# First-tile normalisation on VectorE, spread modulation products and zero matmuls, in the opening of an adaLN + linear attention + SwiGLU kernel

## The chip, the cores and the metric

The kernel runs on one core of a Trainium2 chip. The metric is the device time of one execution in microseconds (us), as a median over runs. The span of a profile, counted from its first instruction, is 1.7 to 2.1 us shorter than the time of the same execution. For most runs the span and the mean granted TensorE clock (as the profiler records it: 1.0 is full speed, 0.5 half) were recorded too.

A ratio of two kernels below is the mean time of one kernel's fast runs over that of the other's of the same rounds, so it is not quite the ratio of the medians that are quoted. "Fast" is a coarse label here: a run is called slow only from 1.5% above the fastest.

## The reference, cut to what matters

```python
mod = (_silu(c) @ w_mod).reshape(c.shape[0], 6, 1, -1)
sa, ca, ga, sb, cb, gb = (mod[:, 0].copy(), mod[:, 1].copy(), ...)
h = _layernorm(x, axis=-1) * (1 + ca) + sa      # x: 1 x 2048 x 1024, bf16
x = x + ga * _A_ref(h, A_wqkv, A_wo)            # q, k, v projections, linear attention, wo
h = _layernorm(x, axis=-1) * (1 + cb) + sb
x = x + gb * _B_ref(h, B_w_gate, B_w_up, B_w_down)
```

Only the first lines matter: before the first key projection, a row tile of `x` must be normalised, transposed and modulated with `ca` and `sa`, and those two are themselves products of a weight that has to be loaded.

## The kernel before: the parts the change touches

The first 512 rows are four row tiles of 128. Each gets statistics on VectorE (`ln_stats`), two small operations on GpSimd, a normalisation (`ln_xn`), eight transposes on TensorE (`tr0`), an evacuation (`tr0_evac`, a copy of the result out of PSUM, where the matmuls write) and a modulation on VectorE (`modulate`).

```python
def ln_xn(st, pool):
    rstd, nmr = stat.pop(st)
    if pool:
        nc.gpsimd.tensor_scalar(out=xns[st % 6], in0=xs[st % 6], scalar1=rstd[:], scalar2=nmr[:], ...)
    else:
        nc.scalar.activation(out=xns[st % 6], in_=xs[st % 6], func=ACT.Identity, scale=rstd[:], bias=nmr[:])
```

`ca` and `sa` are made in four blocks of two column chunks each ("modulation blocks"). A block is two products of 16 matmuls with one column each, kind 0 for `ca` and kind 1 for `sa`, written to columns of bank 7. Then come three small VectorE copies and the modulation of the two chunks. Only after that may the key matmuls of those chunks run. There are eight chunks (`cc`) and eight key groups; `kmm` is one 128x128 by 128x512 matmul. A zero matmul multiplies zeros; nobody uses its result.

```python
def mod_mm(kind, c0, c1):
    for cc in range(c0, c1):
        o = (2 * cc) + kind
        col = (0 if kind else D) + cc * P
        for j in range(DC):
            nc.tensor.matmul(bank[7][:, o:o + 1], lhsT=wme[:, j, col:col + P], rhs=scT[:, j:j + 1],
                             start=(j == 0), stop=(j == DC - 1))

def mod_pair(p):
    mod_mm(0, 2 * p, 2 * p + 2)
    mod_mm(1, 2 * p, 2 * p + 2)
    mod_rows(2 * p, 2 * p + 2)
...
warm(17)                       # zero matmuls, to raise the clock
for st in range(STC):
    ln_stats(st)
...
ln_xn(0, False); tr0(0); warm(3)
ln_xn(1, False); tr0(1); tr0_evac(0)
ln_xn(2, False); ln_xn(3, False)
...
tr0_evac(1); mod_pair(0); tr0(2); tr0_evac(2)
for cc in range(2):
    modulate(0, cc, saT, ca1T, 0, 2 * P)
...                            # key matmuls of chunks 0 and 1, tr0(3), mod_pair(1)
for p in (1, 2):
    for cc in (2 * p, 2 * p + 1):
        for g in range(7):
            kmm(bank[g], 0, G[g][0], G[g][1], cc)
            if p == 1 and cc == 3 and g == 2:
                mod_pair(2)
                for c_ in range(4, 6):
                    modulate(0, c_, saT, ca1T)
mod_pair(3)
for cc in range(6, 8):
    modulate(0, cc, saT, ca1T)
...                            # the 22 key matmuls that are left, then the value matmuls
```

The loads of `x` and of the weights go through one queue (SyncE's) in a fixed order: four row tiles, then modulation blocks alternating with key weights. In the timelines each engine runs its instructions in the order of the program.

## Time and profile before

| | us |
|---|---|
| median of 3 runs | 840.76 (840.35 to 841.16) |
| the profiled run itself | 842.11, span 840.2, mean clock 0.998 |
| TensorE busy | 827.6, 99% |
| value matmuls begin | 32.97 |

The page of before, its head and the busy line (engine, busy us, share of the span, instructions):

```profile
span 840.2 us, 10541 instructions
## 1 busy us (share of the span) xinstructions
PE 827.6 (99%) x4144; PEld 389.8 (46%) x4224; DVE 354.4 (42%) x663; ACT 155.0 (18%) x291; POOL 78.9 (9%) x147
```

TensorE is the limit. So a change of the opening is worth what it moves the start of the value matmuls by, and not more.

The chain of waits of before in its first 45 us (start, length, what), in part:

```profile
11.97 8.95 DMA M<-in_w_mod_dram
...
20.96 0.55 PE bank L391 x16
...
23.26 3.85 PE bank L271 x12
```

The chain reaches back from the second product of the third modulation block (20.96) to the load that it needs. The last line is twelve key matmuls that took 3.85 us.

TensorE in before, in order of time, in part. The columns are start, length, engine, line of the kernel, operation, output and inputs, shapes, count, and in brackets the idle time before the group and what ended it. `128x1` are the modulation products, `128x128` the transposes, L271 the key matmuls, L286 the value matmuls.

```profile
start us, us, engine line op out<-in xcount [idle before <-releaser]
...
11.81 1.03 PE L271 MATMUL bank<-M,M 128*128 128x512 bf16 x3
...
17.04 2.33 PE L271 MATMUL bank<-M,M 128*128 128x512 bf16 x10 [0.24 <-DVE M L253]
19.23 0.55 PE L391 MATMUL bank<-scT,M 128*128 128x1 bf16 x16
20.96 0.55 PE L391 MATMUL bank<-scT,M 128*128 128x1 bf16 x16 [1.18 <-DMA M<-in_w_mod_dram]
21.38 1.67 PE L271 MATMUL bank<-M,M 128*128 128x512 bf16 x5
23.26 3.85 PE L271 MATMUL bank<-M,M 128*128 128x512 bf16 x12 [0.22 <-issue]
...
32.97 1.24 PE L286 MATMUL bank<-M,M 128*128 128x512 bf16 x5
```

Matmuls overlap, so a group's length is not its count times the length of one. From group to group, one 512-column matmul takes about 0.216 us at full clock (for example the 22 key matmuls from 28.22 to 32.97, of which the trace has 21 records), and 0.43 us at half clock.

The windows of before around the DMA wait, TensorE alone (window, its length, busy us with instructions, granted clock, DMA share and GB/s):

```profile
core 0: us, PE busy (x), PEclk, DMA share, GB/s
...
18.63:22.04 3.41, 2.23 (x40) 1.00 1.13 326
22.04:25.45 3.41, 3.19 (x9) 0.50 1.07 314
```

One window of 3.41 us at clock 0.50 follows a window in which TensorE was busy for only 2.23 us. Twelve key matmuls at full clock would take about 2.6 us, so this group lost 1.3 us.

### The profile page before, as it was taken

What the parts mean: (1) busy time and instruction counts of PE and PEld (TensorE: products, weight loads), DVE (VectorE), ACT (ScalarE), POOL (GpSimd) and SP (SyncE); (2) the same over time, 40 slices, a digit from 0 to 9 for tenths busy, and PEclk for the clock granted to TensorE, in tenths of its full rate; (3) what the DMA queues carried; (4) which work ended last, traced back from release to release, by engine and by line L of the source; (5) the groups of instructions that cost most, each with busy time, mean ns of one, the idle gap of its engine ahead of it and who ended that gap; (6) DMA issues with size and microseconds to landing.
All of it is one profiled execution on the core that took longest, in us unless ns stands there. A gap on an engine that the chain in (4) does not pass through costs nothing.

```text
span 840.2 us, 10541 instructions
## 1 busy us (share of the span) xinstructions
PE 827.6 (99%) x4144; PEld 389.8 (46%) x4224; DVE 354.4 (42%) x663; ACT 155.0 (18%) x291; POOL 78.9 (9%) x147
## 2 busy tenths in 40 slices
PE   7999999999999999999999999999999999999998
PEld 3454554544444444444444444444444444444445
DVE  4668888788655656635341111111101211111111
ACT  4335533323211111111110001111000111100000
POOL 2034210022122323100000000000000000000000
PEclk9999999999999999999999999999999999999999
DMA  9985879055599889777874225555322555211210
GB/s 289 312 165 103 161 139 237 17 151 134 127 225 221 219 233 292 187 251 226 249 245 140 76 69 151 151 151 151 106 75 82 154 157 153 76 36 46 76 69 26
DMA packets 223009, 128.62 MB, mean 153 GB/s; under 512 B 76016, under 2 KB 209136, under 8 KB 222960
## 3 DMA queue, kind: packets, MB, share of 16 engines
q1 hardware_dynamic: 182112, 98.58, 43.0%
q10 hardware_dynamic: 38544, 20.98, 11.1%
q0 software_dynamic: 2304, 8.39, 2.6%
q8 instruction: 33, 0.54, 0.3%
q14 instruction: 16, 0.13, 0.1%
HBM read 97.52 MB, written 12.58 MB: 131 GB/s over the span
## 4 chain that ended last, share of the span: by engine, by line
PE 96%; SPq 1%; DMA 1%; issue 1%; DVE 0%; DVEq 0%
PE bank L562 23%; PE bank L581 23%; PE bank L556 23%; PE bank L513 7%; PE bank L286 7%; PE bank L294 7%; PE bank L271 6%; DMA M<-in_w_mod_dram 1%; PE bank L486 1%; PE bank L303 1%; SPq L148 1%; SPq L145 0%; SPq L140 0%; PE bank L391 0%; PE bank L345 0%
## 5 line engine op out<-in xcount | busy, mean ns | idle before, releaser
L562 PE MATMUL bank<-M,M 128*128 128x512 bf16 x881 | 210.4, 379 | 0.9
L556 PE MATMUL bank<-M,M 128*128 128x512 bf16 x870 | 209.5, 379 | 1.3
L564 DVE TENSOR_TENSOR M<-bank,e 128x512 bf16<-128x512 f32 x112 | 77.4, 691 | 249.3 <-PE bank L562 240.8
L581 PE MATMUL bank<-M,M 128*128 128x512 bf16 (+2 forms) x717 | 147.4, 362 | 0.7
L559 ACT ACTIVATE e<-bank 128x512 f32<-128x512 f32 x112 | 66.8, 598 | 436.2 <-PE bank L556 393.7
L581 PEld LDWEIGHTS <-M 128*128 128x128 bf16 x952 | 90.9, 98 | 102.9
L562 PEld LDWEIGHTS <-M 128*128 128x128 bf16 x896 | 87.7, 98 | 105.7
L556 PEld LDWEIGHTS <-M 128*128 128x128 bf16 x896 | 87.3, 98 | 103.8
L584 DVE TENSOR_TENSOR M<-bank,M 128x512 bf16<-128x512 f32 (+2 forms) x34 | 22.4, 660 | 169.9 <-PE bank L581 169.9
L271 PE MATMUL bank<-M,M 128*128 128x512 bf16 x247 | 58.1, 386 | 1.6 <-DVE M L253 0.6
L513 PE MATMUL bank<-M,M 128*128 128x512 bf16 x254 | 57.8, 379 | 0.1
L294 PE MATMUL bank<-M,M 128*128 128x512 bf16 x250 | 56.7, 379 | 0.3
L286 PE MATMUL bank<-M,M 128*128 128x512 bf16 x251 | 55.8, 379 | 0.3
L266 ACT ACTIVATE e<-bank 128x512 f32<-128x512 f32 x64 | 37.3, 596 | 90.2 <-PE bank L294 50.2
L581 PE MATMUL bank<-M 128*128 128x512 bf16 x218 | 50.3, 379 | 0.2
L268 DVE SCALAR_TENSOR_TENSOR M<-bank,e 128x512 bf16<-128x512 f32 x64 | 44.3, 691 | 3.9
L267 DVE TENSOR_SCALAR e<-e 128x512 f32<-128x512 f32 x64 | 29.4, 460 | 23.0 <-ACT e L266 23.0
L271 PEld LDWEIGHTS <-M 128*128 128x128 bf16 x256 | 24.7, 99 | 30.8 <-issue 2.3
L286 PEld LDWEIGHTS <-M 128*128 128x128 bf16 x256 | 25.0, 98 | 30.0
L513 PEld LDWEIGHTS <-M 128*128 128x128 bf16 x256 | 25.0, 98 | 29.7
L294 PEld LDWEIGHTS <-M 128*128 128x128 bf16 x256 | 24.6, 98 | 27.9
L325 DVE CUSTOM_DVE_ANT_0 M<-M,sc_bc 128x1024 f32<-128x1024 bf16 x24 | 29.8, 1241 | 0.5
(84 smaller groups left out, 357.8 us busy)
## 6 DMA issues: line engine op xcount, KB each, us to landing
M<-in_B_w_gate_dram SPq DMA_DIRECT2D x56, 512.0 KB, 3.9
M<-in_B_w_up_dram SPq DMA_DIRECT2D x56, 512.0 KB, 5.1
x_scratch<-M POOLq DMA_DIRECT2D x16, 512.0 KB, 5.8
M<-x_scratch ACTq DMA_DIRECT2D x16, 512.0 KB, 3.4
M<-in_B_w_down_dram SPq DMA_DIRECT2D x6, 1024.0 KB, 8.1
M<-in_A_x_dram SPq DMA_DIRECT2D x16, 256.0 KB, 3.8
M<-in_w_mod_dram SPq DMA_DIRECT2D x8, 512.0 KB, 7.8
M<-in_A_wqkv_dram SPq DMA_DIRECT2D x4, 1024.0 KB, 10.3
```

The lines of the kernel that those rows point to most:

```text
L266: nc.scalar.activation(out=e[:], in_=acc, func=ACT.Exp)
L268: nc.vector.scalar_tensor_tensor(out=dst, in0=acc, scalar=0.0, in1=e[:], op0=ALU.max, op1=ALU.add)
L271: nc.tensor.matmul(acc[:], lhsT=M4[:, sc_, cc, t * P:(t + 1) * P], rhs=wk[:, cc, h * NB:(h + 1) * NB], start=(cc == 0), stop=(cc == DC - 1))
L286: nc.tensor.matmul(acc[:], lhsT=M4[:, sc_, cc, t * P:(t + 1) * P], rhs=wv[:, cc, h * NB:(h + 1) * NB], start=(cc == 0), stop=(cc == DC - 1))
L294: nc.tensor.matmul(acc[:], lhsT=wq[:, cc, qc * P:(qc + 1) * P], rhs=M4[:, sc_, cc, :], start=(cc == 0), stop=(cc == DC - 1))
L325: nc.vector.tensor_tensor_reduce(out=prod.rearrange("p (j k) -> p j k", j=DC), in0=rowT[i][:, :, b, :], in1=sc_bc[:].rearrange("p (j k) -> ...
L513: nc.tensor.matmul(acc[:], lhsT=oTs[st % 3][:, cc, :], rhs=wo[:, cc, hs], start=(cc == 0), stop=(cc == DC - 1))
L556: nc.tensor.matmul(g_ps[:], lhsT=wg_blk[:, cc, fs], rhs=M4[:, sc_, cc, :], start=(cc == 0), stop=(cc == DC - 1))
L559: nc.scalar.activation(out=sg[:], in_=g_ps[:], func=ACT.Silu)
L562: nc.tensor.matmul(u_ps[:], lhsT=wu_blk[:, cc, fs], rhs=M4[:, sc_, cc, :], start=(cc == 0), stop=(cc == DC - 1))
L564: nc.vector.tensor_tensor(out=gus[sc_][:, f, :], in0=u_ps[:], in1=sg[:], op=ALU.mult)
L581: nc.tensor.matmul(y_ps[:, 0:w], lhsT=gus[sc_][:, f, t * P:(t + 1) * P], rhs=wd(f)[:, c0:c1], start=(f == 0), stop=(f == FC - 1))
```

## The change

The intent is to shorten the opening. VectorE normalises faster than ScalarE, so the first row tiles should be ready earlier; in return ScalarE evacuates three of four tiles. The kind-0 product of a block is moved ahead, between key matmuls, and zero matmuls fill the waits so that the clock does not fall. Cut to its core:

```diff
-        if pool:
-            nc.gpsimd.tensor_scalar(...)
-        else:
-            nc.scalar.activation(out=xns[st % 6], in_=xs[st % 6], func=ACT.Identity, scale=rstd[:], bias=nmr[:])
+        eng.tensor_scalar(out=xns[st % 6], in0=xs[st % 6], scalar1=rstd[:], scalar2=nmr[:],
+                          op0=ALU.mult, op1=ALU.add)
@@ tr0_evac
-        if st % 2 == 0:
+        if st < 3:
             nc.scalar.copy(out=dst, in_=tp)
@@
+    def fill(n):
+        for _ in range(n):
+            nc.tensor.matmul(bank[7][:, 64:NB], lhsT=zt[:, 0:P], rhs=zt[:, 0:NB - 64], start=True, stop=True)
@@ the opening (cut; the mask's memsets now stand ahead of it)
-    for st in range(STC):
-        ln_stats(st)
-    ln_xn(0, False)
+    ln_stats(0)
+    ln_stats(1)
+    ln_xn(0, nc.vector)
     tr0(0)
-    warm(3)
-    ln_xn(1, False)
+    tr0_evac(0)
+    warm(4)
+    ln_stats(2)
+    ln_xn(1, nc.vector)
     tr0(1)
+    tr0_evac(1)
+    ln_stats(3)
+    ln_xn(2, nc.vector)
+    mod_pair(0, 0)
+    mod_pair(0, 1)
+    tr0(2)
+    tr0_evac(2)
+    modulate_pair(0, 0, 2 * P)
+    ln_xn(3, nc.vector)
@@ the blocks (the loops of before taken out; kblk(gs, cc) is one kmm per group in gs)
+    kblk(range(4), 0)
+    tr0(3)
+    tr0_evac(3)
+    modulate_pair(0, 2 * P, 4 * P)
+    kblk(range(4), 1)
+    kblk(range(4, 7), 0)
+    mod_pair(1, 0)
+    kblk(range(4, 7), 1)
+    mod_pair(1, 1)
+    modulate_pair(1)
+    fill(2)
+    kblk(range(7), 2)
+    kblk(range(3), 3)
+    mod_pair(2, 0)
+    kblk(range(3, 7), 3)
+    fill(4)
+    mod_pair(2, 1)
+    modulate_pair(2)
+    fill(3)
+    kblk(range(7), 4)
+    mod_pair(3, 0)
+    kblk(range(7), 5)
+    mod_pair(3, 1)
+    modulate_pair(3)
```

More of the change, by code (lines that the diff above doesn't have):

```diff
@@ L232, in ln_stats_act, with ln_xn @@
         stat[st] = (rstd, nmr)
-    def ln_xn(st, pool):
+    def ln_xn(st, eng):
         rstd, nmr = stat.pop(st)
-        if pool:
-            nc.gpsimd.tensor_scalar(out=xns[st % 6], in0=xs[st % 6], scalar1=rstd[:], scalar2=nmr[:],
-                                    op0=ALU.mult, op1=ALU.add)
-        else:
-            nc.scalar.activation(out=xns[st % 6], in_=xs[st % 6], func=ACT.Identity, scale=rstd[:], bias=nmr[:])
+        eng.tensor_scalar(out=xns[st % 6], in0=xs[st % 6], scalar1=rstd[:], scalar2=nmr[:],
+                          op0=ALU.mult, op1=ALU.add)
     def ln(st):
@@ L246, in ln @@
             ln_stats(st)
-        ln_xn(st, True)
+        ln_xn(st, nc.gpsimd)
         sc_, t = divmod(st, STC)
@@ L397, in mod_rows, with mod_pair, modulate_pair @@
         nc.vector.tensor_scalar_add(out=ca1T[:, c0:c1], in0=m1[:, 1, c0:c1], scalar1=1.0)
-    def mod_pair(p):
-        mod_mm(0, 2 * p, 2 * p + 2)
-        mod_mm(1, 2 * p, 2 * p + 2)
-        mod_rows(2 * p, 2 * p + 2)
+    def mod_pair(p, kind):
+        mod_mm(kind, 2 * p, 2 * p + 2)
+        if kind:
+            mod_rows(2 * p, 2 * p + 2)
+    def modulate_pair(p, c0=0, c1=SCW):
+        for cc in (2 * p, 2 * p + 1):
+            modulate(0, cc, saT, ca1T, c0, c1)
     warm(17)
-    for st in range(STC):
-        ln_stats(st)
     mask = const.tile([P, KVW], BF16, name="mask")
@@ L413 @@
     nc.gpsimd.memset(v_c[:, :, :, P:VW], 1.0)
-    ln_xn(0, False)
+    ln_stats(0)
+    ln_stats(1)
+    ln_xn(0, nc.vector)
     tr0(0)
-    warm(3)
-    ln_xn(1, False)
+    tr0_evac(0)
+    warm(4)
+    ln_stats(2)
+    ln_xn(1, nc.vector)
     tr0(1)
-    tr0_evac(0)
-    ln_xn(2, False)
-    ln_xn(3, False)
+    tr0_evac(1)
[7 more added lines that the diff above has]
+    ln_xn(3, nc.vector)
     load_cols(wv, 2 * D, 0)
@@ L427, with kblk @@
     load_cols(wq, 0, 1)
-    tr0_evac(1)
-    mod_pair(0)
-    tr0(2)
-    tr0_evac(2)
-    for cc in range(2):
-        modulate(0, cc, saT, ca1T, 0, 2 * P)
     G = [(t, h) for t in range(STC) for h in range(NH)]
-    for cc in range(2):
-        for g in range(4):
+    def kblk(gs, cc):
+        for g in gs:
             kmm(bank[g], 0, G[g][0], G[g][1], cc)
-        if cc == 0:
-            tr0(3)
-            tr0_evac(3)
-            for c_ in range(2):
-                modulate(0, c_, saT, ca1T, 2 * P, 4 * P)
-    for cc in range(2):
-        for g in range(4, 7):
-            kmm(bank[g], 0, G[g][0], G[g][1], cc)
-        if cc == 0:
-            mod_pair(1)
-            for c_ in range(2, 4):
-                modulate(0, c_, saT, ca1T)
-    for p in (1, 2):
-        for cc in (2 * p, 2 * p + 1):
-            for g in range(7):
-                kmm(bank[g], 0, G[g][0], G[g][1], cc)
-                if p == 1 and cc == 3 and g == 2:
-                    mod_pair(2)
-                    for c_ in range(4, 6):
-                        modulate(0, c_, saT, ca1T)
-    mod_pair(3)
-    for cc in range(6, 8):
-        modulate(0, cc, saT, ca1T)
+    kblk(range(4), 0)
[22 more added lines that the diff above has]
+    modulate_pair(3)
     spread(nc.vector, scT[:])
```

## The prediction

> **What bounds the kernel now.** TensorE: the page's busy table gives it 827.6 of 840.2 us (99%). The change touches only the time before the value matmuls begin, at 32.97 us in the timeline. They follow the key matmuls, so what the opening gains or loses goes one for one into the total.
>
> In that opening the chain of waits holds one DMA wait, ending at 20.92 us (third modulation block). There TensorE idles 1.18 us (timeline), and the clock windows show the granted clock at 0.5 from 22.0 to 25.4 us: 12 key matmuls take 3.85 us where 12 x 0.2145 is 2.57, so 1.3 us is lost. "TensorE: Matmul & The Clock Gate", section Part 1, says the clock is judged in windows of about 3.4 us; the length of this stretch agrees.
>
> **What the change removes, adds and moves.**
> - It removes four ScalarE normalisations (1.24 us each). On VectorE I estimate 0.55 us each, from modulations of 256 and 512 columns (0.34 and 0.41 us).
> - Evacuation of row tile 1 moves from VectorE (0.69) to ScalarE (0.99), off the chain.
> - But VectorE works in order and is the limit here already: four blocks of statistics at 1.63 us, and normalisations now stand between them. My estimate: first transposes 7.5 us (was 7.78), second 9.6 (9.32), third 11.7 (11.36), first key matmul 12.3 (11.81), second half modulated 15.0 (14.53). The opening gets 0.3 to 0.5 us later.
> - With the products spread, no key work covers the chain product, row copies, modulation, matmul (0.9 us) after the second block: key chunk 2 starts at 18.2 instead of 17.04.
> - The DMA wait then vanishes: TensorE reaches that product at about 22.4, by way of four more key matmuls and four zero matmuls. Those are no longer in a wait; they cost about 0.75 us.
> - The third block's latency (0.9 us) loses its cover too.
> - The gain: the half-clock stretch (1.3 us) should go, as TensorE is nearly full from 18 us on.
>
> Sum from 22.4 us: product 0.5, latency 0.9, 14 key matmuls 3.0, last block 0.94 and 0.34, 22 key matmuls 4.7: value matmuls start at about 32.9, against 32.97. A tie, if the clock stays full.
>
> **A risk.** Between 8.4 and 11.8 us TensorE will have less work than before (about 1.9 us of stream against 2.3; 2.0 in the stretch that preceded the drop at 22 us). If that window is judged idle, the first key matmuls and the fourth transposes run at half clock until 15.2, about 1.0 us more. I hold this likelier than not.
>
> **Predicted time:** 841.0 us, range 839.6 to 842.2 (8 in 10). Faster by over 2%: 0.01; within 2%: 0.98; slower: 0.01.
>
> **What would show each step.** Timeline: normalisation near 0.55 us on VectorE; second and third transposes 0.3 us later; chunk 2 near 18.2; no DMA wait of TensorE on modulation blocks. Clock windows: no half clock at 22 to 25 us; possibly one at 12 to 15. Value matmuls starting between 32.3 and 34.0, and from there to the end 807 us in both.
>
> **What would make it wrong.** Normalisation much off 0.55 us; the clock windows lying elsewhere in the run, so that neither or another stretch falls to half clock; the third block's product reached before its DMA lands, which makes the zero matmuls free and the change worth about 1 us; a late landing of the last key weights, binding at 29 us in both kernels.

## The result, and the profile after

| | median | range | runs |
|---|---|---|---|
| before | 840.62 us | 840.22 to 841.16 | 6 |
| after | 843.24 us | 841.96 to 843.55 | 6 |

The ratio is 1.0029 (95% interval 1.0016 to 1.0042): 2.6 us slower, and outside the predicted range of 839.6 to 842.2. Yet both *profiles* show a span of 840.2 us. The resolution is in the list of single runs. The profiled run of after was its fastest: 841.96 us, span 840.2, clock 1.000. The other five took 843.15 to 843.55 us, spans 841.4 to 841.7, clock 0.998. The profiled run of before was longer than every timed run of before. So the two profiles at hand are an unlucky one of before and a lucky one of after.

The page of after:

```profile
span 840.2 us, 10548 instructions
...
PE 828.0 (99%) x4154; PEld 390.5 (46%) x4234; DVE 355.5 (42%) x666; ACT 151.4 (18%) x288; POOL 79.9 (10%) x147
```

TensorE in after, lines that answer to those of before (L268 key, L283 value matmuls, L393 the zero matmuls):

```profile
9.61 0.62 PE L373 MATMUL bank<-ident,M 128*128 128x128 bf16 x8 [0.60 <-DVE M L236]
...
11.69 0.62 PE L373 MATMUL bank<-ident,M 128*128 128x128 bf16 x8 [0.68 <-DVE M L236]
12.43 1.04 PE L268 MATMUL bank<-M,M 128*128 128x512 bf16 x3
...
18.31 2.33 PE L268 MATMUL bank<-M,M 128*128 128x512 bf16 x9
...
21.74 0.92 PE L393 MATMUL bank<-M 128*128 128x448 bf16 x4
22.50 0.54 PE L388 MATMUL bank<-scT,M 128*128 128x1 bf16 x16
23.36 0.73 PE L393 MATMUL bank<-M 128*128 128x448 bf16 x3 [0.32 <-DVE saT L397]
23.95 1.68 PE L268 MATMUL bank<-M,M 128*128 128x512 bf16 x6
...
33.01 1.24 PE L283 MATMUL bank<-M,M 128*128 128x512 bf16 x5
```

Two normalisations on VectorE in after:

```profile
9.01 0.54 DVE L236 TENSOR_SCALAR M<-M,rstd,nmr 128x1024 bf16<-128x1024 bf16 x1
...
11.09 0.54 DVE L236 TENSOR_SCALAR M<-M,rstd,nmr 128x1024 bf16<-128x1024 bf16 x1
```

Read as a schedule at full clock, this is what the prediction drew: normalisation 0.54 us (predicted 0.55), second transposes 9.61 (9.6), third 11.69 (11.7), first key matmul 12.43 (12.3), key chunk 2 at 18.31 (18.2), no DMA wait on a modulation block, value matmuls at 33.01 (32.9). The Trainium skill bears on both durations. "ScalarE: Activation LUTs", section "What ACT_TABLE_LOAD costs", gives 186 ns plus 0.833 ns per element, and about 93 ns for each pointer operand: 1.23 us as an estimate from that page for 1024 elements and two pointers, and the trace of before has 1.24. "VectorE: DVE Perf Modes", section "The perf-mode tier table", has `tensor_scalar` in bf16 from SBUF in its fastest mode, 693 ns at 2048 elements; that table has no figure for 1024, where the trace has 0.54 us.

The chain of waits of after passes through the four zero matmuls that were meant for the wait at 21 us:

```profile
21.90 0.76 PE bank L393 x4
22.66 0.39 PE bank L388 x16
...
23.07 0.16 DVE m L396
```

The product behind them starts at once when they are done. No load is waited for any more, so these 0.76 us are time on the chain and not time in a wait.

### The profile page after: what moved, and what is told of

Read it like the earlier page. It is cut to its first block, busy times and chain, and to the rows that moved or that the text cites. A ratio compares the mean times of both kernels' runs of the same rounds, so it can differ in the third digit from the quotient of the medians.

```text
span 840.2 us, 10548 instructions
## 1 busy us (share of the span) xinstructions
PE 828.0 (99%) x4154; PEld 390.5 (46%) x4234; DVE 355.5 (42%) x666; ACT 151.4 (18%) x288; POOL 79.9 (10%) x147
## 4 chain that ended last, share of the span: by engine, by line
PE 97%; DVE 2%; issue 1%; DMA 0%; DVEq 0%
PE bank L572 23%; PE bank L591 23%; PE bank L566 23%; PE bank L523 7%; PE bank L283 7%; PE bank L291 7%; PE bank L268 7%; PE bank L496 1%; PE bank L300 1%; DVE stats L206 1%; DMA M<-in_A_x_dram 0%; PE bank L388 0%; PE bank L393 0%; DVE M L236 0%; DVE M L250 0%
## 5 line engine op out<-in xcount | busy, mean ns | idle before, releaser
L268 PE MATMUL bank<-M,M 128*128 128x512 bf16 x247 | 57.1, 379 | 1.4 <-DVE M L250 0.4
L283 PE MATMUL bank<-M,M 128*128 128x512 bf16 x251 | 55.8, 379 | 0.3
L283 PEld LDWEIGHTS <-M 128*128 128x128 bf16 x256 | 25.0, 98 | 29.9
L268 PEld LDWEIGHTS <-M 128*128 128x128 bf16 x256 | 24.2, 98 | 29.3 <-DVE M L250 1.9
```

Of the source, the lines that this page charges most:

```text
L268: nc.tensor.matmul(acc[:], lhsT=M4[:, sc_, cc, t * P:(t + 1) * P], rhs=wk[:, cc, h * NB:(h + 1) * NB], start=(cc == 0), stop=(cc == DC - 1))
L283: nc.tensor.matmul(acc[:], lhsT=M4[:, sc_, cc, t * P:(t + 1) * P], rhs=wv[:, cc, h * NB:(h + 1) * NB], start=(cc == 0), stop=(cc == DC - 1))
```

## The experiments

The theory to test (theory 1) has two parts. First, the clock is judged in windows of 3.4 us, which fall well in some runs and badly in others, and the two profiles happened to fall on the wrong sides (for before, e1 will show another reason). Second, at full clock the change costs some 1.3 us by its schedule. Rivals: the profiler itself adds the time (rival 1), the opening alone is what costs (2), the zero matmuls are free and needed (3), the uncovered latency after each block is what costs (4). All runs gave correct results. One run of before took 2281 us; it is left out as slow. e1 to e4 shared one chip; e5 to e12 ran on another.

### e1, e2: both kernels once more, unchanged

Edit: none.

> The kernel before, unchanged. Theory 1 (clock): the profile of before (842.11 us with its profile, span 840.2, a half-clock stretch at 22 us) was an untypical run; the timed runs (840.6 us) are 1.3 to 1.5 us shorter because they keep the full clock. Then the runs here fall into two groups, most near 840.6 with a mean granted clock that rounds to 1.000 and a span near 838.9, some near 842.1 with 0.998. Rival 1 (profiling overhead): every run has the half-clock stretch, the profile merely adds about 1.5 us to any kernel; then all runs of both kernels show 0.998, and a profiled run is always longer than an unprofiled one.

Measured: 840.66 us median (840.35 to 841.73). The profiled run took 840.45 us with a span of 838.4 and clock 1.000. This is before as it usually is:

```profile
19.30 0.54 PE L391 MATMUL bank<-scT,M 128*128 128x1 bf16 x16
20.60 0.55 PE L391 MATMUL bank<-scT,M 128*128 128x1 bf16 x16 [0.76 <-DMA M<-in_w_mod_dram]
21.02 4.24 PE L271 MATMUL bank<-M,M 128*128 128x512 bf16 x17
...
31.20 2.97 PE L286 MATMUL bank<-M,M 128*128 128x512 bf16 x13
```

The windows of this run at the same places as above:

```profile
18.63:22.04 3.41, 2.65 (x40) 1.00 1.13 326
22.04:25.45 3.41, 3.33 (x27) 1.00 1.12 329
```

In this run the load landed at 20.60 instead of 20.96, TensorE idled 0.76 us instead of 1.18, the window ahead of 22.04 held 2.65 us of work instead of 2.23, and the clock did not fall. The windows lay alike in both runs, as far as the warm-up tells: its 17 matmuls take 0.43 us each until the clock rises and 0.2145 us afterwards, so the length of that group places the first window's end. It is 5.70 us in both, which gives 4.95 us, and five windows of 3.41 us later 22.0 us. Between these two profiles of before it was thus a load 0.36 us later that went with the fall, and not the place of the windows; no other slow run of before left a profile, so this is one pair and not a test. The value matmuls start at 31.20 us, not 32.97. The key matmuls between the third and the fourth block take from 21.38 to 26.95 in the first profile (5.57 us) and from 21.02 to 25.09 here (4.07 us): the half-clock window cost 1.5 us, and the later load about the rest of the 1.77 us. From there to the end it is 838.4 - 31.20 = 807.2 us, as in both first profiles (840.2 - 32.97 and 840.2 - 33.01). Rival 1 falls: a profiled run can be as short as any other. Of the 33 runs of before with a recorded clock (the 2281 us run aside), five stand at 842.2 to 842.5 us with clock 0.998 and spans of 840.2 to 840.5. Two more, at 841.73 and 841.97, stand at clock 1.000 and are not explained. One run had clock 0.997 and still took only 840.86 us: a low mean clock alone does not make a run long. Where the half-clock stretch lies matters, as e3 shows.

> The changed kernel, unchanged. Theory 1: the profile of after (span 840.2, clock 1.000, no half-clock stretch) was the untypical run; most runs are near 843.2 with clock 0.998, and a profile of such a run shows a half-clock stretch of 3.4 us between 8 and 16 us, key matmuls there at 0.43 us, and the value matmuls starting near 34.3 instead of 33.0 us. Rival 1: the profile shows full clock and the value matmuls at 33.0 again, and the times are 843.2 all the same, so the loss lies where the profile does not show it.

Measured: 841.97 us median (841.89 to 844.68), ratio 1.0017 (1.0004 to 1.0029). Four runs near 841.95 with spans of 840.1 and 840.2, one at 843.22 with clock 0.998, one at 844.68 with 0.996. The groups are as expected, but on this chip most runs fell into the better one. The profile was again of a good run (value matmuls at 32.93), so the half-clock stretch was still not seen.

### e11, e12: after

Edit: none.

> The changed kernel once more, one look, to catch a profile of its slow group. Theory 1: a run near 843.2 us shows a half-clock stretch that begins between 10.5 and 13 us and value matmuls near 34.3 us; a run near 841.9 shows none and 33.0.

Measured: 843.23 us, span 841.4, clock 0.998. TensorE, in part:

```profile
11.69 0.62 PE L373 MATMUL bank<-ident,M 128*128 128x128 bf16 x8 [0.68 <-DVE m L396]
12.43 0.52 PE L268 MATMUL bank<-M,M 128*128 128x512 bf16 x1
13.16 1.06 PE L268 MATMUL bank<-M,M 128*128 128x512 bf16 x2 [0.22 <-issue]
14.02 1.06 PE L373 MATMUL bank<-ident,M 128*128 128x128 bf16 x8
14.87 2.27 PE L268 MATMUL bank<-M,M 128*128 128x512 bf16 x7
...
34.18 2.10 PE L283 MATMUL bank<-M,M 128*128 128x512 bf16 x9
```

And two of its windows, the one ahead of the fall and the one at half clock:

```profile
core 0: us, PE busy (x), PEclk, DMA share, GB/s
9.16:12.57 3.41, 2.16 (x49) 1.00 1.13 322
12.57:15.98 3.41, 3.19 (x14) 0.50 1.13 328
```

Up to the first key matmul this run is the profile of after to a few hundredths of a microsecond. Then the clock falls at 12.57 us for one window. Two key matmuls take 1.06 us, eight transposes 1.06 instead of 0.61, and the value matmuls start at 34.18 instead of 33.01 us. That is 1.2 us, and the span is 1.2 us longer. The window that was judged had 2.16 us of work; its longest waits were 0.60 and 0.68 us. Here the place of the windows makes the difference: by the length of the warm-up (5.35 us in the profile of after, 6.07 here) they end at 7.65 and 11.07 there, and at 9.1 and 12.5 here. Only in the second case does one window hold both waits and little else. In all fourteen profiles, the only half-clock stretches after the warm-up and up to 837 us lie between 10.6 and 25.5 us (before, e3, e6, e11).

> The same once more, with the same expectation: if near 843.2 us, a half-clock stretch in the opening and value matmuls near 34.3 us; if near 841.9 us, none and 33.0.

Measured: 841.95 us, span 840.2, clock 1.000, value matmuls at 32.98: the other group, as expected.

### e3: the opening alone

Edit: the opening of after, followed by the block loops of before.

```diff
     ln_xn(3, nc.vector)
     ...
-    kblk(range(4), 0)
-    tr0(3)
-    ... (the whole block order of after)
+    ... (the block order of before, with mod_pair of before)
```

> Only the first part of the change: normalisation on VectorE, evacuation on ScalarE, memsets and statistics reordered; the block order of before, no zero matmuls in the waits. Theory 1 with the slack in the DMA wait at 20.9 us: the opening is 0.5 us later (first key matmul near 12.4 us), but the DMA wait absorbs it, also most of a half-clock stretch before 15 us: 840.3 to 841.3 us, within 0.1% of before. Rival 2 (the opening is what costs): 842.0 us or more, since everything behind it moves by the 0.5 us plus the half clock.

Measured: 841.05 us median (840.62 to 841.25), ratio 0.9997 (0.9984 to 1.001). Four of five runs had clock 0.997 or 0.998, the profiled one too:

```profile
12.38 0.61 PE L268 MATMUL bank<-M,M 128*128 128x512 bf16 x1
13.21 1.06 PE L268 MATMUL bank<-M,M 128*128 128x512 bf16 x2 [0.22 <-issue]
...
21.03 0.94 PE L388 MATMUL bank<-scT,M 128*128 128x1 bf16 x32
...
31.94 2.32 PE L283 MATMUL bank<-M,M 128*128 128x512 bf16 x10
```

The key matmuls begin about 0.5 us later (12.38 against 11.90 in e1) and then run at half clock until about 15.7 us. Still the value matmuls begin at 31.94, 0.74 us later than in e1. The slack of the DMA wait took up the rest: the third block's products now run as one group of 32 at 21.03 without a wait. Rival 2, in the form that the opening alone makes the loss, falls. With before's block order the later opening and a half-clock window cost about 0.3 us of time (841.05 against 840.72 for before in the same rounds).

### e4: the block order alone

Edit: the opening of before, followed by the block order and the zero matmuls of after.

```diff
     tr0_evac(1)
     mod_pair(0)
     tr0(2)
     tr0_evac(2)
     ...
-    ... (the block order of before)
+    kblk(range(4), 0)
+    ... (the whole block order of after, with fill(2), fill(4), fill(3))
```

> Only the second part: before's opening (normalisation on ScalarE), but products spread between key matmuls and zero matmuls as in after. Theory 1: the uncovered latency and the four zero matmuls put TensorE past the DMA wait: 841.3 to 841.9 us, 0.7 to 1.3 above before, with full clock. Rival 2 (the opening is what costs): as before, 840.6, within 0.3 us.

Measured: 841.50 us median (841.46 to 841.62), all at clock 0.999 or 1.000, ratio 1.0004 (0.9992 to 1.0016). The interval of the ratio is wide because it includes the slow group of before; the five runs of e4 lie within 0.16 us of each other. Value matmuls start at 32.35, 1.15 us later than in e1. The expectation of theory 1 (841.3 to 841.9) holds. Every run keeps the clock. The opening of before holds more matmul work between 8.4 and 11.8 us (2.49 us in e4 against 2.12 in after), which may be why; no run tests it.

### e5: more zero matmuls in the opening of after

```diff
     warm(4)
+    guard(2)          # zero matmuls into bank 0, which the first key matmul overwrites
     ...
     mod_pair(0, 1)
+    guard(3)
     tr0(2)
```

> The changed kernel with five zero matmuls more, two after the warm-up before the second transposes and three before the third, in waits of 0.6 and 0.7 us, into a bank that is overwritten later. Theory 1 (the loss of the 843.2 us runs is an idle-judged clock window of the opening): no run at 843.2 or above is left, all at 841.7 to 842.1 us, profile with full clock from 5 us on and the value matmuls at 32.9 to 33.1. Rival 1 (something that the clock does not explain): runs at 843.2 stay, in about the share seen so far (7 of 12 runs above 843).

Measured: 841.94 us median, and all five runs between 841.88 and 841.98 at clock 1.000. Value matmuls at 32.97. Of 14 runs of after itself, 8 took over 843 us. Five zero matmuls in waits of 0.6 and 0.7 us delay nothing (third transposes at 11.66, first key matmul at 12.40), and no slow run is left. Alone that is thin: of the seven other runs on this chip with after's unguarded opening (e7, e11, e12) only two were slow. With the five of e9, also all at clock 1.000, and the trace of e11, where the half-clock window itself delays the value matmuls by 1.2 us, it shows the slow group of after to be the opening's clock.

### e6: no zero matmuls in the opening after the warm-up

```diff
     tr0_evac(0)
-    warm(4)
     ln_stats(2)
```

> The changed kernel without the four zero matmuls after the first transposes; nothing else touched. Theory 1: TensorE has 0.9 us less work between 8 and 12 us, so the clock window is judged idle in every run: all at 843.0 to 844.7 us, and the profile shows half clock over some 3.4 us beginning between 10 and 13 us, key matmuls near 0.43 us and the value matmuls at 34.2 to 34.6. Rival 1: the zero matmuls lie in a wait, so taking them away changes nothing: 841.9 us with the same mix as before.

Measured: 843.20 us median; 843.94, 843.28, 843.01 and 843.20 at clock 0.996 to 0.998, and one run at 841.94 with clock 1.000. "In every run" was wrong: one of five escaped. The profiled run (843.94) was at half clock from about 10.6 to 17.4 us, the length of two windows, and its value matmuls started at 34.97 instead of the expected 34.2 to 34.6. So two windows in a row can be lost. Four slow runs of five against eight of 14 in after do not by themselves show that taking the zero matmuls away made slow runs more frequent; the judged window of the profile, with 1.66 us of work against 2.16 in e11, fits it. The 844.68 us run of e2, at the same mean clock of 0.996, may be such a case, but it left no profile.

### e7: after without the nine zero matmuls of the blocks

```diff
-    fill(2)
...
-    fill(4)
...
-    fill(3)
```

> The changed kernel without the nine zero matmuls in the waits for modulation blocks (two, four, three). Theory 1: the four before the third block's second product run in no wait and cost 0.76 us, the others run while the modulation is awaited and cost nothing: the fast group moves from 841.95 to 841.2 us, value matmuls at 32.2 in a full-clock profile; a slow group 1.3 us above may stay, since the opening is untouched. Rival 3 (the zero matmuls are free and needed): no gain, 841.9 or more, with a half-clock stretch at 21 to 26 us.

Measured: 841.64 us median (841.21, 841.42, 841.64, 841.68 at clock 1.000; 842.59 at 0.998). Only one of the four full-clock runs came to the expected 841.2. In the profile the schedule moved as expected:

```profile
21.70 0.54 PE L388 MATMUL bank<-scT,M 128*128 128x1 bf16 x16
23.15 1.69 PE L268 MATMUL bank<-M,M 128*128 128x512 bf16 x6 [0.91 <-DVE M L250]
...
32.21 2.10 PE L283 MATMUL bank<-M,M 128*128 128x512 bf16 x9
```

The product follows the last key matmul of chunk 3 directly, and the value matmuls start at 32.21 instead of 33.01. With the zero matmuls gone, TensorE idles 0.91 us after the block instead of multiplying zeros, and the clock held nonetheless. So the four in `fill(4)` cost their 0.76 us, and the other five cost nothing. In this one run 0.46 us were given back at 169.5 us, where a group of eight attention matmuls took 1.09 us instead of 0.63; why, was not found. That run's span was 839.9, so from the value matmuls to the end it took 807.7 us instead of 807.2. The start of the value matmuls is the cleaner evidence here.

### e9: both repairs of after together

```diff
+    guard(2)  ...  +    guard(3)         # as in e5
-    fill(2)   ...  -    fill(4)   ...  -    fill(3)
```

> The changed kernel with the five zero matmuls of the guard in the opening and without the nine in the waits for modulation blocks: both repairs together. Theory 1 with the sizes found: the guard takes away the slow group, the missing four give 0.76 us: value matmuls at 32.2 us, runs between 841.0 and 841.7 us, none above 842.3. Still some 0.6 us behind before, since the opening on VectorE is later and its latency after the blocks is uncovered. Rival 3: a half-clock stretch in the waits without zero matmuls (18 or 22 us) puts runs at 842 to 843.

Measured: 841.19 us median, all five runs between 841.12 and 841.26, clock 1.000, value matmuls at 32.22, ratio 1.0003 (0.9988 to 1.0017). Both effects add: the slow group is gone, and the missing zero matmuls give 0.75 us against e5. Rival 3 falls: no run needed the zero matmuls of the blocks.

### e10: the block order alone, without zero matmuls

```diff
     (e4)
-    fill(2)   ...  -    fill(4)   ...  -    fill(3)
```

> Before's opening, products spread between key matmuls, no zero matmuls in the waits. Theory 1: without the opening's delay and without the zero matmuls the third block's second product is reached at 21.1 us, next to the landing of its DMA; value matmuls at 31.5 to 31.7, 840.5 to 840.9 us, so spreading by itself is neutral. Rival 4 (the uncovered latency after each block is what costs): 841.3 us or more, as with the zero matmuls.

Measured: 840.85 us median (840.76 to 840.97), all at clock 1.000; before in the same rounds 840.53 median. The profile:

```profile
21.08 0.54 PE L391 MATMUL bank<-scT,M 128*128 128x1 bf16 x16
22.53 1.69 PE L271 MATMUL bank<-M,M 128*128 128x512 bf16 x6 [0.91 <-DVE M L253]
...
31.59 4.70 PE L286 MATMUL bank<-M,M 128*128 128x512 bf16 x21
```

One of its windows, which held little work and did not cost the clock:

```profile
14.20:17.61 3.41, 2.25 (x38) 1.00 1.15 320
```

The third block's second product is reached at 21.08, about when its load lands. Value matmuls at 31.59, against 32.35 in e4. So 0.65 us of e4's 841.50 (0.76 us at the start of the value matmuls) were the zero matmuls. Rival 4 falls as the main cause: the latency, 0.91 us twice in this profile, is mostly time that before spends in the DMA wait. Spreading by itself is nearly neutral, some 0.3 us behind before.

### e8: before, with zero matmuls in its waits

```diff
     warm(3)
+    guard(1)
     ...
     mod_pair(0)
+    guard(2)
     tr0(2)
@@ mod_pair(p)
         mod_mm(0, 2 * p, 2 * p + 2)
+        if p == 2:
+            fill(3)
         mod_mm(1, 2 * p, 2 * p + 2)
```

> The kernel before with six zero matmuls more: one and two in waits of the opening, three in the DMA wait before the third block's second product. Theory 1: the runs of before at 842.4 (3 of 11 on the last chip) are gone, all at 840.3 to 840.8 us; no gain on its fast runs, since the DMA wait still ends at 20.6 to 21 us. Rival 1: the share at 842.4 stays.

Measured: 840.37 us median (840.06 to 841.35), all at clock 1.000, ratio 0.9998 (0.9985 to 1.001). No run fell to half clock, but one stood at 841.35 at full clock, unexplained, outside the expected 840.3 to 840.8. Before itself had no run at 842 in those rounds, so this does not show that the guard helps; it shows no cost beyond the noise. No version was found that clearly beats before.

## Why the prediction was wrong

The time fell outside the range, 1.0 us above its upper end. Point by point:

**The step that failed is the baseline.** The prediction says "value matmuls start at about 32.9, against 32.97. A tie, if the clock stays full", and books "The gain: the half-clock stretch (1.3 us) should go". Both take the profile of before for the runs that make up its median. The half-clock stretch was in the profiled run (842.11 us, 1.35 us above the median). The clock of the timed runs of that session was not recorded, but their times (840.22 to 841.16) lie where the runs of e1 that kept it mostly lie (840.35 to 840.86), and below all of the slow group (842.2 and more). In e1 the value matmuls of before start at 31.20 us, and spans of 838.4 to 838.8 us put them at 31.2 to 31.6 in most runs (an estimate: the span less 807.2). So the usual run had no 1.3 us to gain, and against 31.2 to 31.6 the start at 33.0 is a loss of 1.4 to 1.8 us (1.25 us in time, e2's median against before in its rounds). The hint was in the data: a profiled run 1.35 us above a median whose three runs differ by 0.8 us.

**The schedule of after was right** at every point named above, within 0.15 us, from the normalisation's 0.55 to the value matmuls' 32.9. The zero matmuls were "about 0.75 us" in the text; e7 and e9 give 0.75 to 0.80 in the start of the value matmuls.

**The risk was right in mechanism and nearly in size.** The text says that the window between 8.4 and 11.8 us "is judged idle", which costs "about 1.0 us more". e11 shows the half clock about 0.8 us later than drawn, from 12.57 to 15.98 us, and a loss of 1.2 us; e5 and e9 show that it is the cause. The place came from the profile of before, and it differs from run to run: the warm-up lasts from 5.13 to 6.80 us in the fourteen profiles. The text held this risk "likelier than not", yet its 841.0 us lies only 0.24 us above the median of before, so little of the loss is in the number. The list of what would make it wrong did name "the clock windows lying elsewhere in the run". The prediction also said "half clock at 22 to 25 us" should go. That is right of after, but most runs of before do not have it either.

The sum, in medians of time (chips differ between the rows, so each step has an error of 0.1 to 0.2 us):

| step | kernel | us | step |
|---|---|---|---|
| before | | 840.6 | |
| products spread, latencies uncovered | e10 | 840.85 | +0.25 |
| zero matmuls in the blocks | e4 | 841.50 | +0.65 |
| opening with normalisation on VectorE, clock held | e5 | 841.94 | +0.44 |
| its clock window judged idle (8 of 14 runs) | e11, one run | 843.23 | +1.29 |

The total of 2.6 us is the measured difference of the first session, in which five of six runs of after were in the slow group (clock 0.998, as in e11). On the chip of e2 it was 1.3 us.

**What stays open.** In span the opening costs 0.6 to 0.7 us (e4 to e5, 839.5 to 840.2; e10 to e9, 838.8 to 839.4), in time only 0.34 to 0.44: the kernels with the new opening have about 0.2 us less between span and time. Not explained are also why the window's place favours one group on one chip and the other on another, and the three full-clock runs of before and of e8 at 841.35 to 841.97 us.

## What to carry to other kernels

Before a difference of less than half a per cent is drawn from a profile, compare the profiled run's own time with the timed runs: a profile is one run, and this kernel, where one window of the opening keeps or loses the clock, has two kinds of run. Zero matmuls were worth placing where TensorE truly waits and the load of a 3.4 us window is low (e5); once an earlier part of the same change has made the wait vanish, they are plain work on the chain (0.76 us here). Moving an operation to a faster engine (0.54 us instead of 1.24) gained nothing here, as the chain already passed through that engine: the second transposes came 0.3 us later.

## What the Trainium skill lacked or had wrong

- "TensorE: Matmul & The Clock Gate", Part 1, "What's actually happening", says that the clock falls after an idle window of about 3.4 us, and "HAM oscillation — how this bites in real kernels" gives "no PE-idle gaps >~3.4µs" as the rule. In the fourteen profiles the full-clock windows followed by half clock held 2.23 (before), 2.1 (e3, e11) and 1.7 us (e6) of busy time out of 3.41, and none of them a gap above 1.5 us. Full-clock windows from 2.25 us (e10) upwards kept the clock. (Where no fall marks the windows, their places are an estimate from the length of the warm-up, good to about 0.1 us.) A limit on a single gap does not fit: e3 and e11 lost the clock with no gap above 0.68 us, and e7 kept it with one of 0.91. A share of busy time, near two thirds as this profile counts it, sorts all of them; but 2.23 and 2.25 are closer than the windows can be placed, and no run separates busy time from other measures of work. The page gives no such limit. The same number does not hold at half clock: in e6 a half-clock window with 2.52 us of busy time was followed by another, while those with 3.09 us (e3) and more were followed by full clock.
- The same page's remark that the window is free-running, and does not start with the kernel, agrees: the warm-up lasts from 5.13 to 6.80 us in the fourteen profiles, and after has two groups of runs 1.3 us apart. The page draws from this only that the warm-up varies; that a fall after it can come and go in the same way, as in 8 of 14 runs of after, it does not say.
- That page does not say whether matmuls of zeros count as work for the clock gate. They do: the 17 of the warm-up raise it in all fourteen profiles, and five in the opening held the clock at 1.000 in ten of ten runs (e5, e9), where after without them lost it in 8 of 14.
